# Loading two rows of an output projection through GpSimd's queue, in pieces of 57 and 38 partitions

## The chip, the core and the metric

The kernel runs on one core of one Trainium2 chip. The metric is the device time of one execution in microseconds; the time of the kernel before is the median of three runs. A core has five engines that matter here: TensorE (PE), VectorE (DVE), ScalarE (ACT), GpSimd (POOL) and SyncE (SP). Transfers between the chip's memory (HBM) and the core's memory (SBUF) are made by sixteen DMA engines; a transfer is put into a queue by an instruction on SP, ACT or POOL.

## The reference

Grouped-query attention of 8 sequences with 4 new tokens each, against caches of 2,048 keys and values, between two projections. All inputs are bf16.

```python
B, Sq, D = 8, 4, 512
Hq, Hkv, Sk, Dh = 32, 8, 2048, 128
# x (B,Sq,D)  k_cache, v_cache (B,Hkv,Sk,Dh)  wq (D,Hq*Dh)  wo (Hq*Dh,D)
q = (x @ wq).reshape(B, Sq, Hq, Dh).transpose(0, 2, 1, 3)
k = jnp.repeat(k_cache, Hq // Hkv, axis=1)
v = jnp.repeat(v_cache, Hq // Hkv, axis=1)
scores = jnp.einsum("bhqd,bhkd->bhqk", q, k) * (Dh ** -0.5)
o = jnp.einsum("bhqk,bhkd->bhqd", softmax(scores), v)
out = o.transpose(0, 2, 1, 3).reshape(B, Sq, Hq * Dh) @ wo
```

The caches are 32 MB (of 1,048,576 bytes) each, wq and wo 4 MB each, so that nearly all of the traffic is read once.

## The kernel before

The work is cut into eight units, u = 0 to 7. A unit is 4 MB of keys and 4 MB of values: units 1 to 6 are one sequence with all its eight heads, units 0 and 7 are half of the heads of the last two sequences. SBUF holds a ring of four slots of 4 MB (`ring`, 128 partitions of 32 KB in each slot). All large loads go into the ring in a fixed order: k0, wq, k1, v0, k2, v1, k3, v2 and so on to v6, v7, wo. `take` deals the slots round, so wo, the eighteenth load, gets the slot that v5 had.

For one unit, DVE transposes the keys (`turn`, L213), PE multiplies them with the queries (`scores`, L251), DVE finds the maximum (L264), ACT takes the exponentials (L291), DVE transposes them (L305), and ACT and POOL copy them into a block-diagonal tile (`p_bd`, L315). One unit later PE multiplies these with the values (`values`, L331). In the program's order, pass u of the main loop (L442) holds the scores of unit u and the values of unit u - 1, and ends with `issue(2 + 2 * u)` (L472), which puts into the queues the loads whose slots are free by then. The transfer that follows in a queue waits, on the issuing engine, until the last reader of its slot is done. Pass 6 issues wo, so wo waits for `values(5, 1)`.

The loads are issued by SP, but for one half of k0, which is issued by ACT. `load_kv` (L110) makes one DMA of a whole 4 MB unit, or two. A unit named in the list `split` (L155) is cut by member, that is into the two halves of each partition's 32 KB in SBUF; for values these are two groups of four heads. v7 is cut another way, into halves of the keys. A V load cut by member and a whole one read the same runs of 16 KB in HBM.

`load_wo` (L141) sees wo as two halves, gg = 0 and 1, each of 128 partitions with sixteen rows of 512 numbers (1 KB a row, so 16 KB in one run for each partition). The first half is one DMA of sixteen rows; the second is cut into rows 0 to 7, 8 to 12, 13 to 14, and 15.

At the end `project` (L399) multiplies the attention's result with wo, row by row, two matmuls for a row: the first half's rows 0 to 3, then its rows 4 to 15, then the second half's rows 0 to 15 (L476 to L480). Each row waits for the DMA that brought it. The result is then copied by DVE and ACT (L482, L483) and stored by SP (L484).

The tile `pad` (128 partitions of 192 numbers, L72) stands ahead of the ring in SBUF. The kernel before neither writes nor reads it.

Of the kernel before, what the change touches and what calls it, by code (L numbers as in the profile page):

```python
# [17 lines left out]
def kernel(  # L18
# [9 lines left out]
    nc = tc.nc  # L28

    B, Sq, D = x.shape  # L30
# [11 lines left out]
    NU = B * Hkv // (G * NB)  # L42
# [11 lines left out]
    RW = 16  # L54
# [17 lines left out]
    pad = ring_pool.tile([128, 192], BF16, name="pad")  # L72
    ring = ring_pool.tile([128, NR, NB, C * Dh], BF16, name="ring")
# [27 lines left out]
    def take(key):  # L101
        slot_of[key] = n_loads[0] % NR
        n_loads[0] += 1
        return slot_of[key]
# [30 lines left out]
    def load_wq():  # L135
# [2 lines left out]
            ring[:, slot, :, :].rearrange("p b n -> p (b n)"), wq.rearrange("(p r) n -> p (r n)", r=R)  # L138
        )

    def load_wo():  # L141
        slot = take("wo")
        for gg, cuts in ((0, (0, RW)), (1, (0, 8, 13, 15, RW))):
            rows = wo[gg * G * 512 : (gg + 1) * G * 512, :].rearrange("(p r) j -> p (r j)", r=RW)
            for r0, r1 in zip(cuts, cuts[1:]):
                nc.sync.dma_start(ring[:, slot, gg, r0 * D : r1 * D], rows[:, r0 * D : r1 * D])

    loads = ["k0", "wq", ("k", 1)]
    for u in range(NU):
# [2 lines left out]
            loads.append(("k", u + 2))  # L152
    loads.append("wo")
    loads.reverse()
    split = [("v", 0), ("v", 1), ("v", 2), ("v", 3), ("v", 4), ("k", NU - 1)]  # L155

    def issue(done):

        while loads and n_loads[0] < done + NR:
            what = loads.pop()  # L160
            if what == "k0":
                load_kv("k", 0, by_member, (nc.sync, nc.scalar))
                nc.sync.dma_start(x_sb[:, :], x.flatten_outer_dims())
            elif what == "wq":
                load_wq()
            elif what == "wo":
                load_wo()
            elif what in split:
                load_kv(*what, by_member)
            else:  # L170
                load_kv(*what, by_half if what == ("v", NU - 1) else whole)
# [343 lines left out]
```

## Time and profile before

| what | value |
|---|---|
| median of three runs | 184.73 us (184.65 to 189.89) |
| the profiled execution, own time | 184.38 us |
| its span, first to last instruction | 182.5 us |
| mean granted TensorE clock | 0.963 |
| PE, DVE, ACT, POOL busy | 136.6, 128.7, 70.3, 39.3 us |
| moved by DMA | 75.70 MB, mean 415 GB/s |
| chain that ended last | DMA 42%, DVE 23%, PE 22% |

All times in the views are of the profiled execution, in microseconds from the start of its span. A DMA is cut into packets, one for each contiguous run of one partition; the packets are dealt to the DMA engines. The trace has, for each packet, its queue, size, start and duration, and for each DMA the sixteen times at which its completion semaphore was raised, without the engine's name. The packets of kind "instruction" bring instructions to the engines' own memories; the kernel does not issue them. Queue 1 is SP's.

### The profile page before, as it was taken

To read this page: it belongs to the slowest core of one execution; us is meant where nothing else is said; L and a number is where in the kernel's file an instruction comes from. 1 tells how busy PE (TensorE), PEld (TensorE's weight loads), DVE (VectorE), ACT (ScalarE), POOL (GpSimd) and SP (SyncE) were. 2 spreads that over 40 slices of the span, in tenths; PEclk is the share of its full clock that TensorE was granted. 3 is DMA by queue.
4 is the path that set the end of the run, shared out by engine and by line. 5 is a ranking of instruction groups with operands and counts; after the bars stand their busy time and mean duration, and the time that the engine had idled before them with its cause. 6 is when DMAs were issued, how large, how long until landed. Compare 5 with 4: busy or idle time off the path is not lost.

```text
span 182.5 us, 2386 instructions
## 1 busy us (share of the span) xinstructions
PE 136.6 (75%) x924; PEld 83.3 (46%) x924; DVE 128.7 (71%) x161; ACT 70.3 (39%) x91; POOL 39.3 (22%) x110
## 2 busy tenths in 40 slices
PE   0000076940999999998999898989399977899993
PEld 0000022310348635843783485358234852388971
DVE  6518025738994999599689957995399559967340
ACT  2000020019604940990395079109900792063010
POOL 8800006006200700430080035004400220023000
PEclk9999999995589999999999999999969999999999
DMA  6999999999999998999999999999999999999991
GB/s 226 431 485 395 424 460 406 424 445 449 452 384 427 456 461 382 420 460 452 391 417 453 460 402 418 431 478 424 391 435 424 435 427 435 415 426 438 427 385 42
DMA packets 4938, 75.70 MB, mean 415 GB/s; under 512 B 512, under 2 KB 704, under 8 KB 960
## 3 DMA queue, kind: packets, MB, share of 16 engines
q1 hardware_dynamic: 4784, 73.47, 94.3%
q10 hardware_dynamic: 144, 2.10, 2.8%
q8 instruction: 7, 0.11, 0.2%
q14 instruction: 3, 0.02, 0.0%
HBM read 75.53 MB, written 0.03 MB: 414 GB/s over the span
## 4 chain that ended last, share of the span: by engine, by line
DMA 42%; DVE 23%; PE 22%; issue 4%; ACT 3%; POOL 2%; SPq 1%; ACTq 0%; DVEq 0%; POOLq 0%
DMA ring<-in_wo_dram 16%; PE s_ps L251 16%; DMA ring<-in_k_cache_dram 15%; DVE kt L213 14%; DMA ring<-in_wq_dram 12%; DVE stat L264 4%; PE o_ps L331 4%; ACT p_sb L291 3%; PE psq L425 2%; DVE pt L305 2%; DVE stat L322 1%; POOL p_bd L315 1%; POOL q_bd L231 1%; PE s_ps L403 1%; DVE stat L272 0%
## 5 line engine op out<-in xcount | busy, mean ns | idle before, releaser
L251 PE MATMUL s_ps<-kt,q_bd 128*128 128x512 bf16 x256 | 69.5, 409 | 20.0 <-POOL q_bd L231 9.9
L213 DVE STREAM_TRANSPOSE kt<-ring 128x1024 f32<-128x1024 f32 x64 | 73.9, 1210 | 14.2 <-DMA ring<-in_k_cache_dram 11.4
L331 PE MATMUL o_ps<-ring,p_bd 128*128 128x256 bf16 x512 | 57.2, 273 | 0.0
L251 PEld LDWEIGHTS <-q_bd 128*128 128x128 bf16 x256 | 25.3, 102 | 63.0 <-issue 26.6
L331 PEld LDWEIGHTS <-p_bd 128*128 128x128 bf16 x512 | 49.8, 98 | 6.0 <-issue 0.2
L315 ACT COPY p_bd<-pt 32x1024 bf16<-32x1024 bf16 x44 | 45.8, 1041 | 1.5 <-DVE pt L305 1.1
L291 ACT ACTIVATE p_sb<-s_ps,stat 128x1024 bf16<-128x1024 f32 x16 | 17.7, 1110 | 72.2 <-DVE stat L272 72.2
L315 POOL COPY p_bd<-pt 32x1024 bf16<-32x1024 bf16 x16 | 17.0, 1065 | 105.9 <-DVE pt L305 93.2
L264 DVE TENSOR_REDUCE stat<-s_ps 128x1 f32<-128x1024 f32 x16 | 19.3, 1208 | 3.4 <-PE s_ps L251 3.4
L305 DVE STREAM_TRANSPOSE pt<-p_sb 128x512 f32<-128x512 f32 x16 | 11.4, 712 | 14.0 <-ACT p_sb L291 14.0
L231 POOL COPY q_bd<-qT 32x64 bf16<-32x64 bf16 x64 | 13.1, 231 | 20.7 <-DVE qT L436 19.0
L425 PE MATMUL psq<-ring,xT_sb 128*32 128x512 bf16 x32 | 3.6, 630 | 9.1 <-DMA ring<-in_wq_dram 9.1
L416 PE MATMUL xtp<-ident,x_sb 32*128 32x32 bf16 x4 | 0.3, 195 | 13.3 <-DMA x_sb<-in_x_dram 13.3
L436 DVE STREAM_TRANSPOSE qT<-q_sb 128x64 f32<-128x64 f32 x8 | 1.2, 214 | 8.8 <-ACT q_sb L432 8.8
L177 DVE MEMSET p_bd<- 128x2048 uint32 x3 | 5.3, 1765 | 2.0 <-PEq L499 1.2
L322 DVE TENSOR_SCALAR stat<-of_b,stat 128x2 f32<-128x2 f32 x8 | 6.3, 793 | 0.3
L416 PEld LDWEIGHTS <-x_sb 32*128 32x128 bf16 x4 | 0.2, 117 | 13.3 <-DMA x_sb<-in_x_dram 13.3
L425 PEld LDWEIGHTS <-xT_sb 128*32 128x32 bf16 x32 | 1.3, 140 | 10.5 <-issue 10.1
L432 ACT CAST q_sb<-psq 128x512 bf16<-128x512 f32 x2 | 1.2, 586 | 11.8 <-PE psq L425 11.8
L375 PEld LDWEIGHTS <-perm 128*128 128x128 bf16 x56 | 3.8, 97 | 2.0 <-issue 0.5
L419 ACT COPY xT_sb<-xtp 128x128 bf16<-128x128 bf16 x1 | 0.3, 266 | 11.2 <-PE xtp L416 11.2
L343 ACT ACTIVATE o_sb<-o_ps,stat 128x128 bf16<-128x128 f32 x8 | 2.9, 368 | 4.1 <-PE o_ps L331 3.9
(30 smaller groups left out, 46.4 us busy)
## 6 DMA issues: line engine op xcount, KB each, us to landing
ring<-in_k_cache_dram SPq DMA_DIRECT2D x6, 4096.0 KB, 22.7
ring<-in_v_cache_dram SPq DMA_DIRECT2D x12, 2048.0 KB, 23.6
ring<-in_v_cache_dram SPq DMA_DIRECT2D x2, 4096.0 KB, 29.6
ring<-in_k_cache_dram SPq DMA_DIRECT2D x3, 2048.0 KB, 27.2
ring<-in_wq_dram SPq DMA_DIRECT2D x1, 4096.0 KB, 21.0
ring<-in_k_cache_dram ACTq DMA_DIRECT2D x1, 2048.0 KB, 12.4
ring<-in_wo_dram SPq DMA_DIRECT2D x1, 2048.0 KB, 25.9
ring<-in_wo_dram SPq DMA_DIRECT2D x1, 1024.0 KB, 28.2
```

The source lines that it names most:

```text
L177: nc.vector.memset(t[:, :, :, :, :], 0.0)
L213: nc.vector.transpose(out=out, in_=in_)
L231: nc.gpsimd.tensor_copy(out=qb[k * 32 : (k + 1) * 32, m, :, g, b, :].rearrange("w (j e) q -> w j e q", e=2), in_=qT[of * 32 : (of + 1) * 3 ...
L251: nc.tensor.matmul(s_ps[t // 2][:, t % 2, :], lhsT=q_bd[u % 2][:, m, 2 * j + e, :, :, :].rearrange("w g b q -> w (g b q)"), rhs=rhs, start ...
L264: nc.vector.tensor_reduce(out=stats[u][0][:, h : h + 1], in_=s_ps[h][:, :, :].rearrange("q t n -> q (t n)"), axis=AX, op=ALU.max, negate=True,
L291: nc.scalar.activation(out=out, in_=in_, func=EXP, bias=stats[u][1][:, :], scale=scale, accum_out=stats[u][2][:, h : h + 1],)
L305: nc.vector.transpose(out=pt[:, :, :, :].rearrange("s c q e -> s (c q e)").bitcast(FP32), in_=ps[u, h][:, :, :, :].rearrange("q c s e -> q ...
L315: copy(out=pb[rows, :, g, :, :], in_=pt[rows, :, :, :])
L322: nc.vector.tensor_scalar_mul(stats[u][3][:, :], of_b[:, :], stats[u][4][:, :])
L331: nc.tensor.matmul(o_pss[u][:, :, :], lhsT=pbs[u, h][:, i // 2, :, :, i % 2].rearrange("s g q -> s (g q)"), rhs=v[:, :, key_of(u, h, i // ...
L375: nc.tensor.matmul(o_pms[r // 2][:, r % 2, gg, :], lhsT=perm[:, r, w : w + 128], rhs=o_sbs[u][:, b, :], start=(u == 0 and r % 2 == 0 and g ...
L425: nc.tensor.matmul(psq[g * T : (g + 1) * T, :], lhsT=xT_sb[:, r, :], rhs=w[:, (g * NB + gg) * rep * Dh : (g * NB + gg + 1) * rep * Dh], st ...
```

## The change

The first half of wo is no longer one DMA. Rows 0 to 13 are loaded by SP as before. Rows 14 and 15, which make one run of 2 KB for each partition, are cut by partitions: 0 to 56 (57 partitions) and 57 to 94 (38) are issued by GpSimd, 95 to 126 (32) and 127 (one) by SP. Ahead of each GpSimd piece stands a short load by GpSimd too, `load_rows`, of 6 and of 5 rows of x with 24 bytes each, into `pad`, which still nobody reads. The second half is cut as before. Also v3 and v4 leave the list `split`, so that each of them is loaded by one DMA of 4 MB instead of two of 2 MB.

```diff
+    def load_rows(n):
+
+        nc.gpsimd.dma_start(pad[:n, 16 * n : 16 * n + 12], x.flatten_outer_dims()[:n, :12])
+
     def load_wo():
         slot = take("wo")
-        for gg, cuts in ((0, (0, RW)), (1, (0, 8, 13, 15, RW))):
+
+        def load(engine, gg, p0, p1, r0, r1):
             rows = wo[gg * G * 512 : (gg + 1) * G * 512, :].rearrange("(p r) j -> p (r j)", r=RW)
-            for r0, r1 in zip(cuts, cuts[1:]):
-                nc.sync.dma_start(ring[:, slot, gg, r0 * D : r1 * D], rows[:, r0 * D : r1 * D])
+            engine.dma_start(ring[p0:p1, slot, gg, r0 * D : r1 * D], rows[p0:p1, r0 * D : r1 * D])
+
+
+        RL, PA, PB = RW - 2, 57, 57 + 38
+        load(nc.sync, 0, 0, 128, 0, RL)
+        load_rows(6)
+        load(nc.gpsimd, 0, 0, PA, RL, RW)
+        load_rows(5)
+        load(nc.gpsimd, 0, PA, PB, RL, RW)
+        load(nc.sync, 0, PB, PB + 32, RL, RW)
+        load(nc.sync, 0, PB + 32, 128, RL, RW)
+        for r0, r1 in ((0, 8), (8, 13), (13, 15), (15, RW)):
+            load(nc.sync, 1, 0, 128, r0, r1)
...
-    split = [("v", 0), ("v", 1), ("v", 2), ("v", 3), ("v", 4), ("k", NU - 1)]
+    split = [("v", 0), ("v", 1), ("v", 2), ("k", NU - 1)]
```

## The prediction

> **What bounds the kernel now.** I read the page's slices and queues first, then the chain that ended last, then the timeline of the last 35 us, and last the completion records.
>
> The page's DMA lines (busy tenths in 40 slices; then queue, packets, MB, share of 16 engines' span):
>
> ```profile
> span 182.5 us, 2386 instructions
> PE   0000076940999999998999898989399977899993
> DMA  6999999999999998999999999999999999999991
> q1 hardware_dynamic: 4784, 73.47, 94.3%
> q8 instruction: 7, 0.11, 0.2%
> ```
>
> The DMA engines are full from the second slice to the last but one; SP's queue q1 fills nearly all of that. No other row is as full.
>
> The chain that ended last (start us, us, what), its end:
>
> ```profile
> 148.45 0.34 SPq L146
> 148.79 0.05 issue
> 148.84 0.42 SPq L146
> 149.27 0.05 issue
> 149.32 29.10 DMA ring<-in_wo_dram
> 178.42 0.04 issue
> 178.46 0.27 PE s_ps L403
> ...
> 179.71 0.40 DVE out_sb L482
> ```
>
> The wo pieces are issued from 148.45 and land up to 29 us later: they stand behind a backlog, so when they are issued matters little, and what the engines still have to move matters. In the timeline (start us, us, engine, line) POOL has little there:
>
> ```profile
> 144.77 2.14 POOL L315 COPY p_bd<-pt 32x1024 bf16<-32x1024 bf16 x2 [14.49 <-DVE pt L305]
> 163.22 1.23 POOL L315 COPY p_bd<-pt 32x1024 bf16<-32x1024 bf16 x1 [16.31 <-DVE pt L305]
> ...
> 178.46 0.27 PE L403 MATMUL s_ps<-ring,oP 128*32 128x256 bf16 x1 [0.34 <-DMA ring<-in_wo_dram]
> ...
> 180.17 0.35 SPq L484 DMA_DIRECT2D out_dram<-out_sb  x1
> ```
>
> PE reaches row 8 of wo's second half and waits for a transfer; POOL is idle from 146.9 to 163.2.
>
> Each load leaves sixteen completion marks in the trace, one for each DMA engine, without the engine's name. For the last wo load (row 15 of the second half), us after the first mark at 177.54:
>
> ```
> 0 .19 .37 .38 .44 | .66 .67 .78 .81 | 1.50 1.52 1.65 1.66 1.77 1.79 1.81
> ```
>
> The last comes at 179.35, PE's last matmuls start at 179.39, and the span ends 3.1 us after that mark. So **five engines lead, four are between, seven lag**, and the seven decide. Where they come from is in the same records: up to 51.7 us the spread is 0.7 us; each of the seven 16 KB records of q8 (starting 53.9, 74.8, 93.5, 116.4, 139.7, 163.3 and 175.0) is followed by one more engine that stays about 1.1 us behind (1 at 57.6, 2 at 77.3, 4 at 120.8, 7 at 179.35). No engine is hit twice.
>
> **What each part costs.** SP's packets in the steady stretch take 611 ns for 16,384 B, 309 for 8,192, 196 for 5,120, 84 for 2,048, 46 for 1,024 and 9 for a 4 B mark: 8 ns and 36.8 ns per 1,000 B. A packet of 14,336 B then is 536 ns.
>
> - Shortening the first half's load from sixteen rows to fourteen: each engine has 8 of its 128 packets, so 8 x (611 - 536) = -0.60 us on every engine.
> - The load of 32 partitions: 2 packets of 2,048 B on each engine, 2 x 84 = +0.17. x, also 32 rows, left 2 packets for each of 16 marks. The load of one partition is +0.08 on one engine.
> - The GpSimd pieces, 57 and 38 packets of 2,048 B. No row shows a load from this queue. The rows of SP's loads are dealt in equal shares (128 as 16 x 8, 32 as 16 x 2). Equal shares of 57 on at most 16 engines means 1 or 3 engines, and of 38 it means 1 or 2; as many as possible gives 3 and 2, **nineteen packets each, 19 x 84 = +1.60 on five engines**. The bounds are 4 + 3 packets on nearly every engine (+0.59) and all 57 on one engine (+4.79); I take nineteen as nearest to the even dealing of the rows.
> - The short loads of x: 6 and 5 packets of 24 B, at most 46 ns each by the nearest row; +0.02 on eleven engines. Dealt in turn, 6, 3, 5 and 2 engines make sixteen, so no engine gets two pieces. Their data goes into pad, which nobody reads.
> - Marks: four GpSimd loads, 4 x 9 = +0.04. The two V loads whole instead of split save 2 x 9 ns, the two new SP loads add 2 x 9. The packets of these V loads stay 16 KB and both members are read by the same matmuls, so else it is nothing.
>
> Sum: the eleven other engines -0.60 + 0.17 + 0.04 + 0.02 = -0.38; the five -0.60 + 0.17 + 0.04 + 1.60 = +1.20.
>
> On the spread, if the five are the leaders: 0 to .44 become 1.20 to 1.64, the laggards 1.43 at most, the middle 0.43. The last mark moves from 1.81 to 1.64: **-0.17 us**. PE passes this on: its waits for wo after 177.85 add up to more (0.34 us before 178.46 alone).
>
> The Trainium skill's page "DMA: Bandwidth & Descriptors", section "Why a DMA increments its semaphore by 16 and not by 1", gives the same 3 and 2 (the largest divisor up to 16) and lets GpSimd's queue deal to consecutive engines from a cursor that goes round; no run here shows it yet. The same sentence speaks of an exception, a rival below.
>
> **What lies beside other work.** SP issues seven wo loads instead of five and two fewer V loads; two issues of 0.4 us are hidden by the 26 to 29 us of backlog. SP's loads use eight semaphores in turn; moved on by the new loads, the last two wo issues would take those of v6 and of v7's first half, which landed at 159.76 and 164.64. If SP waits for them, only the output's DMA is behind (180.17), and the pieces are still 13 us ahead of their landing; with no backlog left this would be on the path whole. POOL gains a **wait** for values(5) to free the slot (PE's last read ends at 148.44), then four issues. Behind it is only the p_bd copy at 163.22, for which values(7) waits; 14.8 us cover it. No row prices a POOL issue; against SP's 0.4 us it would need 3.7 us each to show, so I take nothing; without the cover each us is an us for that copy. The early bytes (190 KB) are moved ahead of v6 and v7. On leaders this only uses up their lead (v6's leaders at 157.89 plus 1.6 is 159.5, before the last mark at 159.76). PE must observe four loads instead of one before rows 14 and 15 of the first half, some tenths of a us at most, covered by the waits it now has at 178.46.
>
> The Trainium skill speaks against such a change in the same page's "Rules for kernel authors": spreading loads over SP, ACT and GpSimd brings no bandwidth, since all use the same sixteen engines. The trace agrees that the engines are full (1.00 from 30 to 165 us); by that rule alone the sum would be zero, since it is about the total and not about who is late.
>
> **Rivals.** (1) *The five engines are not the leaders.* The marks don't name engines, and five drawn blindly from sixteen would avoid all seven laggards in 126 of 4,368 draws. Then a laggard ends at 1.50 + 1.20 = 2.70 to 1.81 + 1.20 = 3.01: +0.9 to +1.2 us, 185.3 to 185.6, and v6 and v7 land as much later. It decides as soon as one engine at 0.61 or later is among the five (0.61 + 1.20 = 1.81). Against it: the extra of 1.60 is near the distance between the groups (means 0.28 and 1.67), and the short loads can serve nothing but the choice of engines. Should the fetches or the dealing start elsewhere from run to run, this is the usual case.
> (2) *The pieces go evenly over the engines.* 4 + 3 packets: -0.60 + 0.17 + 0.04 + 0.59 = +0.20, 184.6. The exception named above (the Trainium skill, same section: some plain GpSimd copies get 16 engines with the rounded-up share) would do just this. The rows of 128 and 32 can't tell it from equal shares, but they don't show an uneven share either.
> (3) *One engine takes a whole piece.* -0.38 + 4.79 = +4.41 on one engine: 0.44 + 4.41 - 1.81 = +3.0 on a leader, +4.4 on the last laggard: 187.4 to 188.8. For it: nothing but that no row excludes it.
> (4) *A GpSimd issue costs far more than SP's* and p_bd's copy comes late: from 14.8 us on, us for us. A lead of 0.7 us (everything levelled at the mean of 1.00 plus 0.11) is the most that the other side could give: 183.7.
>
> **How the numbers follow.** The sum is made against the profiled execution's own 184.38 us (span 182.5 and 1.9 around it), 0.35 below the median of 184.73. Forecast 184.38 - 0.17 = **184.2**, chance 0.55, its own range 183.8 to 184.6 (packets on the new queue 20% dearer add 0.3; full levelling takes 0.5 more). Rival 1 at 0.28, 2 at 0.08, 3 at 0.05, 4 and the rest at 0.04. From 183.8 to 185.6 holds forecast and rivals 1 and 2 but for their edges. A measurement of this kernel can tell about 2% from no change, 3.7 us. Over 2% slower takes rival 3 on a late engine or rival 4: 0.05. Over 2% faster nothing here gives; 0.02 for what I don't see. Within 2%: 0.93.
>
> **What would show it.** Right: the last load's marks no longer fall in groups of five, four and seven but within some 1.2 us with four at the front; the four POOL loads issued between 148.5 and 155 and landed before 160; the POOL copy still at 163; the tail of 3.1 us after the last mark unchanged. Wrong: two or more marks over 2.5 us behind the first (rival 1), the old groups with all of them 0.2 later (2), one mark 4 us behind (3), or values(7) waiting for POOL (4).

## The result and the profile after

The changed kernel takes **185.75 us** (median), the kernel before 184.71 in the same comparison; the ratio is 1.0055, with a 95% interval of 1.0042 to 1.0068. That is 1.0 us slower: within 2%, but clear of noise, on the other side of the forecast of 184.2 and just above the range. In a second comparison of the same kernel the ratio was 1.0144 (1.0126 to 1.0162), 2.6 us.

The first profile after the change is of an execution of 191.93 us, in which packets were slower between 13 and 66 us already; so the lines below are from the second profile of the same kernel (187.14 us), and of four experiments (wo alone, no short loads, the pieces by SP, the even pieces by SP) only the times from 140 us on are used. First what the DMA engines moved in the 40 slices of the kernel before:

```profile
GB/s 226 431 485 395 424 460 406 424 445 449 452 384 427 456 461 382 420 460 452 391 417 453 460 402 418 431 478 424 391 435 424 435 427 435 415 426 438 427 385 42
```

and the page after the change (the slices, then the queues):

```profile
span 185.3 us, 2393 instructions
DMA  6999999999999999999999999999999999999991
GB/s 223 439 471 439 425 396 435 435 460 439 393 421 442 467 433 387 425 460 439 400 432 432 446 419 425 471 410 417 439 421 428 439 415 406 376 386 396 364 361 38
q1 hardware_dynamic: 4802, 73.27, 94.0%
q0 software_dynamic: 160, 0.20, 0.3%
```

The DMA engines are as full as before, and the bytes are the same, but from the 34th slice on they move less: 361 to 406 GB/s, where the kernel before has 385 to 438. q0 is GpSimd's queue. The windows of the same stretches show when that begins (us from the start, the engines' busy time, granted clock, DMA share, GB/s); the kernel before:

```profile
142.00:152.00 10.00, 7.89 (x66) 6.25 (x65) 6.06 (x10) 8.81 (x11) 2.08 (x2) 1.00 1.01 431
152.00:162.00 10.00, 9.16 (x54) 4.65 (x53) 8.90 (x10) 0.93 (x1) 0.00 (x0) 1.00 0.99 422
162.00:172.00 10.00, 10.00 (x98) 9.02 (x96) 6.28 (x12) 4.19 (x8) 2.45 (x2) 1.00 1.03 435
172.00:177.00 5.00, 4.65 (x59) 3.80 (x58) 2.12 (x6) 0.74 (x2) 0.00 (x0) 1.00 0.97 401
```

and the changed kernel:

```profile
142.00:152.00 10.00, 7.89 (x67) 6.37 (x66) 6.05 (x10) 8.80 (x11) 4.23 (x6) 1.00 1.02 434
152.00:162.00 10.00, 7.91 (x42) 3.40 (x40) 9.14 (x10) 0.69 (x1) 0.00 (x0) 1.00 0.99 386
162.00:172.00 10.00, 10.00 (x95) 8.96 (x94) 5.50 (x10) 4.06 (x7) 2.58 (x2) 1.00 1.03 394
172.00:177.00 5.00, 3.98 (x41) 3.46 (x39) 1.89 (x3) 0.74 (x2) 0.00 (x0) 1.00 1.00 360
```

The DMA share is 1.0 in all of them, so no engine ran dry; each packet took longer. Up to 152 us the two kernels agree (431 and 434 GB/s). The timeline says what starts then (POOL's queue, start and length in us):

```profile
148.97 0.54 POOL L150 DMA_DIRECT2D ring<-in_wo_dram  x1 [1.24 <-PE o_ps L347]
149.50 0.51 POOL L143 DMA_DIRECT2D pad<-in_x_dram  x1
150.00 0.53 POOL L150 DMA_DIRECT2D ring<-in_wo_dram  x1
163.39 1.29 POOL L331 COPY p_bd<-pt 32x1024 bf16<-32x1024 bf16 x1 [12.87 <-DVE pt L321]
```

The first piece of wo is issued at 148.97, its packets run from 152.8. In the packet records SP's packets of 16,384 B take about 681 ns instead of 611 from 157 us on, and those of 8,192 B about 342 instead of 309, up to 177 us. I sum this up as the **excess**: what SP's packets from 140 us on took beyond 8 ns and 36.8 ns per 1,000 B, divided by sixteen engines. It is 0.07 us in the kernel before and 2.49 in this profile. The chain of waits ends as before, only later:

```profile
150.32 30.81 DMA ring<-in_wo_dram
181.13 0.04 issue
181.17 0.27 PE s_ps L419
...
182.39 0.40 DVE out_sb L498
```

The last wo mark comes at 182.03 (before: 179.35), the marks of that load are spread over 1.85 us (before: 1.81), seven engines still lag, and the tail after the last mark is 3.2 us.

### The profile page after: what moved, and what is told of

It reads as the page before. It is cut to its first block, busy times and chain, and to the rows that moved or that the text cites. A ratio compares the mean times of both kernels' runs of the same rounds, so it can differ in the third digit from the quotient of the medians.

```text
span 190.0 us, 2393 instructions
## 1 busy us (share of the span) xinstructions
PE 137.0 (72%) x924; PEld 83.6 (44%) x924; DVE 128.9 (68%) x161; ACT 70.2 (37%) x91; POOL 41.5 (22%) x114
## 4 chain that ended last, share of the span: by engine, by line
DMA 57%; PE 17%; DVE 17%; issue 3%; POOL 2%; ACT 2%; SPq 1%; ACTq 0%; POOLq 0%; DVEq 0%
DMA ring<-in_k_cache_dram 29%; DMA ring<-in_wo_dram 16%; DVE kt L229 13%; DMA ring<-in_wq_dram 12%; PE s_ps L267 10%; PE o_ps L347 4%; PE psq L441 2%; ACT p_sb L307 1%; DVE stat L280 1%; POOL p_bd L331 1%; DVE pt L321 1%; SPq L150 1%; POOL q_bd L247 1%; PE s_ps L419 1%; DVE stat L338 0%
## 5 line engine op out<-in xcount | busy, mean ns | idle before, releaser
L419 PE MATMUL s_ps<-ring,oP 128*32 128x256 bf16 x32 | 4.3, 272 | 0.7 <-DMA ring<-in_wo_dram 0.6
```

Of the source, the lines that this page charges most:

```text
L419: nc.tensor.matmul(out_ps[half], lhsT=oP[gg][:, r, :], rhs=w[:, r, half * DH : (half + 1) * DH], start=(gg == 0 and r == 0), stop=(gg == N ...
```

## The experiments

All ratios are to the kernel before on the same chip, with the 95% interval. The first four ask which part costs.

**The whole change again.** No edit.

> The whole change again, for a profile that can be laid beside the one of before. Packet records of the first profile after the change show the 57 rows dealt as four rows each on fourteen engines and one on a fifteenth, the 38 as three each on twelve and two on one. Theory A (the GpSimd queue is the cost: the pieces are dealt almost evenly, so no laggard is relieved, and the packets and marks of that queue cost more engine time than the 0.20 us of rival 2): about 1.0055, the last wo mark some 1 us later against the start than before, and the delay appears between 150 and 165 us, when that queue's packets run. Theory B (the whole V loads are the cost): the same ratio, but the loads after v3 and v4 already land about 0.8 us later than before, between 90 and 125 us. Theory C (the two last wo loads are issued later because SP waits): the same ratio, with a gap in the DMA engines' work after 175 us.

1.0144 (1.0126 to 1.0162). The landings up to 150 us agree with those of before within 0.3 us, so the whole V loads (theory B) are out. SP's wo issues, before (first line) and in this run (second line):

```profile
148.45 7.75 SPq L146 DMA_DIRECT2D ring<-in_wo_dram  x5
148.58 18.39 SPq L150 DMA_DIRECT2D ring<-in_wo_dram  x7
```

SP now needs 18.39 us to get through them, as the prediction's order of semaphores has it, but there is no gap after 175 us: the pieces still land in order with the engines full, so theory C is out too.

**Only the V loads whole.**

```diff
-    split = [("v", 0), ("v", 1), ("v", 2), ("v", 3), ("v", 4), ("k", NU - 1)]
+    split = [("v", 0), ("v", 1), ("v", 2), ("k", NU - 1)]
```

> Only v3 and v4 are loaded whole; wo as in the kernel before. Theory A: 1.000 (0.999 to 1.001), since the same packets move. Theory B: about 1.0045, +0.8 us, with the landings after v3 later. Theory C: 1.000.

1.0004 (0.9991 to 1.0017). By itself this part is nothing.

**Only wo in the new way.** The change without the edit above.

> Only wo is loaded in the new way; v3 and v4 stay split. Theory A: the whole loss, about 1.0055. Theory B: about 1.001, +0.2 us from the even dealing. Theory C: the whole loss.

1.0084 (1.0066 to 1.0102): the loss is in wo's load. Its excess is 0.88 us, in two stretches: 0.5 while GpSimd's packets run and 0.3 where SP's pieces of 32 and 1 partitions pass. The whole change cost 1.0144 beside it, though the V loads alone cost nothing. Whether the two parts act on each other is not shown: the same whole change gave 1.0055 in the first comparison, so one kernel differs by as much from one comparison to the next.

In this experiment and in all that follow v3 and v4 are split as in the kernel before, and each diff shows only the lines that load rows 14 and 15 of the first half of wo, against the changed kernel or, where it has the loop over `cuts`, against the kernel before.

**The cut without the second queue.**

```diff
-        for gg, cuts in ((0, (0, RW)), (1, (0, 8, 13, 15, RW))):
+        for gg, cuts in ((0, (0, RW - 2, RW)), (1, (0, 8, 13, 15, RW))):
```

> The first half of wo is cut into rows 0 to 13 and rows 14 and 15, both by SP over all 128 partitions: the cut without the other queue; v3 and v4 split. Each engine gets 8 packets of 14,336 B and 8 of 2,048 B for 8 of 16,384 B, 8 x (536 + 84 - 611) ns + one mark = +0.08 us. Theory A and B: 1.0005, all the rest being the queue or the V loads. Theory C: SP issues one load more, so one late issue of the two remains; a part of the loss, about 1.002.

1.0004 (0.9991 to 1.0018), excess 0.07. Shorter packets as such cost what the prediction said, and the stream keeps its rate where these rows pass (172 to 177 us, before 401 GB/s):

```profile
172.00:177.00 5.00, 4.65 (x56) 3.80 (x56) 2.12 (x5) 0.74 (x2) 0.00 (x0) 1.00 0.99 405
```

The packet records of the changed kernel also tell how the pieces were dealt. GpSimd's queue made packets of up to 4,096 B, two rows each, where SP's queue makes one of each row. Of the 57 rows, fifteen engines got their first packet within 1 us; there were 28 packets of two rows and one of a single row, which is four rows on each of fourteen engines and one on a fifteenth. The 38 became 13 packets of two rows and 12 of one: three rows on each of twelve engines, two on another. So at most twelve engines got seven rows, nobody got more, and nobody got nineteen. The next question was what makes the packets slow: a second queue (theory Q) or the shape of the pieces (theory S).

**Without the short loads of x** (wo as in the change, v3 and v4 split, the two `load_rows` calls left out).

> v3 and v4 split as before; wo in the new pieces, but without the two short loads of x. In the profile of the whole change, SP's packets take 10% longer from the moment when GpSimd's queue runs (16,384 B in 681 ns instead of 611), for 24 us; in that of wo alone for shorter stretches. Theory Q (any larger load on a second queue throws the engines' packets out of step, and they stay slow until something puts them back) and theory S (it is the shape of the pieces, whose partitions are dealt to other engines than SP's loads of 128): as wo alone, 1.005 to 1.013. Theory D (the short loads matter, by moving on which engines get the pieces): another loss than that, below 1.003 or above 1.015.

1.014 (1.0026 to 1.0253), a wide interval; excess 0.86, again in two stretches. The short loads are not needed for the loss.

**Only the short loads.**

```diff
         load_rows(6)
-        load(nc.gpsimd, 0, 0, PA, RL, RW)
         load_rows(5)
-        load(nc.gpsimd, 0, PA, PB, RL, RW)
-        load(nc.sync, 0, PB, PB + 32, RL, RW)
-        load(nc.sync, 0, PB + 32, 128, RL, RW)
+        load(nc.sync, 0, 0, 128, RL, RW)
```

> The two short loads of x stay on GpSimd's queue, and rows 14 and 15 of the first half are loaded by SP over all 128 partitions. Theory Q in its strict form (any packet on a second queue does it): a slow stretch, 1.004 or more. Theory Q for larger loads only, and theory S: 1.0005 as with the cut by SP alone.

1.0013 (0.9997 to 1.0029), excess 0.07. The six packets of 24 B of the first short load start at 150.751, .901, .996, 151.078, .113 and .343; the five of the second at 151.977, 152.126, .222, .339 and .569, each 1,225 or 1,226 ns after one of the first six, two of SP's packets later. They went to five of the same six engines: a short load does not move the next one on to other engines.

**GpSimd's queue with an even load of 128 partitions.**

It stands in place of the four pieces and the short loads.

```diff
+        load(nc.gpsimd, 0, 0, 128, RL, RW)
```

> Rows 14 and 15 of the first half are one load of 128 partitions by GpSimd, no short loads: the second queue with the even shape of SP's loads. Engine work: 8 x (536 - 611) + 4 x 168 ns + marks = +0.1 us. Theory Q: SP's packets slow down beside and after it, 1.004 to 1.013. Theory S: 1.001.

1.0002 (0.9989 to 1.0015): **a second queue alone costs nothing.** Its 64 packets of 4,096 B took 159 ns each, excess 0.08, and the windows are those of before (422 and 435 GB/s):

```profile
152.00:162.00 10.00, 8.56 (x48) 4.04 (x47) 9.07 (x10) 0.76 (x1) 0.00 (x0) 1.00 0.99 422
162.00:172.00 10.00, 10.00 (x98) 9.02 (x96) 5.69 (x11) 4.36 (x8) 2.58 (x2) 1.00 1.03 434
```

Theory Q is out.

**The pieces by ACT's queue** (`nc.scalar` for `nc.gpsimd`, no short loads).

> The pieces of 57 and 38 partitions are issued by ACT instead of GpSimd, no short loads. If this queue deals equal shares (nineteen packets on each of three and of two engines), and always from the same first engine on, two engines get both pieces: -0.40 + 3.20 = +2.8 us on them, so 1.4 us (on leaders) to 2.8 us (on laggards) later, 1.008 to 1.015; if it deals like GpSimd's, 1.001 and what theory Q or S add. Theory Q and S both expect SP's packets to be slow beside it; only theory Q expects them to stay slow after it.

1.0194 (1.0117 to 1.0272). Three engines had one of these packets every 687 ns, in three phases that stay fixed up to 156 us, and each got nineteen: this queue does deal equal shares, and the 38 went to two engines. In the last load's marks two engines stand 3.1 and 3.6 us behind the first, the others within 2.0. The excess of 1.83 us comes on top and begins only about 157 us, after several rounds.

Three more kernels separate the shares from the partitions.

**The same pieces, all by SP** (`nc.sync`, no short loads).

> The pieces of 57, 38, 32 and 1 partitions are all issued by SP, no second queue and no short loads. ACT's queue dealt the 57 as nineteen packets on each of three engines and the 38 on two of the same engines. If SP's deals alike, two engines have 2.8 us more, as with ACT. Theory U (uneven shares move the engines' packets against each other, and then they run slower, whatever the queue): slow stretches without any second queue, 1.012 to 1.02. Theory Q2 (uneven pieces do it only beside another queue): SP's packets keep 611 and 309 ns, and only the engine work is left, 1.007 to 1.010.

1.0178 (1.0115 to 1.0242), excess 1.40 in one stretch of about 5 us; the 2,048 B packets took up to 155 ns instead of 84. No second queue is needed for slow packets. The page counts 534 packets under 512 B, 22 more than before. These are the marks of the four pieces, 16 + 3 + 2 + 1, so SP's queue dealt the 57 to three engines and the 38 to two, as ACT's did.

**Even pieces, by SP and by GpSimd.** The lines by SP, in place of the four pieces and the short loads; in the second kernel `nc.gpsimd` issues the first of the two.

```diff
+        load(nc.sync, 0, 0, 96, RL, RW)
+        load(nc.sync, 0, 96, 128, RL, RW)
```

> Rows 14 and 15 by SP in pieces of 96 and 32 partitions: 6 + 2 packets on every engine, an even share, but with other partitions on an engine than in a load of 128. Engine work as with the plain cut, +0.09 us with one more mark. Theory U: 1.0005, no slow stretch. Theory M (the other partitions do it: two engines meet at one place in SBUF or HBM): a slow stretch of about 10% while these packets run, some 0.1 us in 1 us, and as long after as it stays; 1.001 to 1.005.

> As the even pieces by SP, but the 96 partitions are issued by GpSimd: 6 packets on each engine, beside v6. Theory U: about 1.0005, like GpSimd's load of 128, and SP's packets keep their 611 ns but for some tens of ns. Theory M: slow while the 96 packets run, 10% or more over 3 us, 0.3 us or more, 1.002 to 1.008.

1.0072 (1.0043 to 1.0101) by SP and 1.0070 (1.0041 to 1.0099) with the 96 by GpSimd. **Theory U is out: both pieces have marks from all sixteen engines (544 packets under 512 B, 32 more than before), so the shares are even, and the packets are slow all the same.** By SP the excess is 0.96 us, all of it while these 128 packets run: 84 ns for the first 59 of them, then up to 162. By GpSimd it is 1.29: 0.59 beside the 96 (153 to 156 us) and 0.65 from 173 to 178 us, where the 32 pass. In between, the packets have their old times, as the windows of this kernel show:

```profile
152.00:162.00 10.00, 8.73 (x42) 3.98 (x41) 8.90 (x10) 0.79 (x1) 0.00 (x0) 0.83 0.99 393
162.00:172.00 10.00, 10.00 (x97) 9.00 (x95) 5.50 (x10) 3.96 (x7) 2.58 (x2) 1.00 1.02 430
172.00:177.00 5.00, 4.65 (x52) 3.78 (x49) 1.89 (x3) 0.75 (x3) 0.00 (x0) 1.00 1.01 377
```

393 GB/s beside the 96, 430 without a piece, 377 beside the 32.

**All partitions, other rows of HBM.** Rows 14 and 15 in one SP load, in place of the four pieces and the short loads. Partition 8b + a gets the wo rows of partition 16a + b, so the result is a sum over other rows than the reference's:

```diff
+        turned = wo[: G * 512, :].rearrange("(a b r) j -> b a (r j)", b=16, r=RW)
+        nc.sync.dma_start(
+            ring[:, slot, 0, RL * D : RW * D], turned[:, :, RL * D : RW * D]
+        )
```

> Rows 14 and 15 of the first half are one SP load into all 128 partitions, but partition 8b + a takes the wo rows that belong to partition 16a + b, so the result is a sum over other rows than the reference's. SBUF is written in an even load over all partitions, HBM is read in another order by each engine. Theory M on the HBM side (an engine that reads other addresses than in a load of 128 meets another engine's): the 2,048 B packets take 100 to 160 ns instead of 84 and the loss is as with the even pieces by SP, 1.004 to 1.007. Theory M on the SBUF side (two engines write to partitions that lie together): 84 ns and 1.0004, as with the plain cut, as long as engine and partitions stay paired as in a plain load.

1.0085 (1.0068 to 1.0102). Even shares, all 128 partitions, and still 84 ns turned into up to 208, excess 1.19:

```profile
162.00:172.00 10.00, 10.00 (x98) 9.01 (x97) 6.09 (x12) 4.34 (x8) 2.45 (x2) 1.00 1.02 430
172.00:177.00 5.00, 4.30 (x51) 3.50 (x50) 1.75 (x4) 0.74 (x2) 0.00 (x0) 1.00 1.00 323
```

323 GB/s where the kernel before has 401. This speaks for the HBM side, but it does not settle it. The edit also moves the rows that neighbouring partitions read from 16 KB to 256 KB apart, which the pieces do not, so its slow packets may have another cause than theirs. The Trainium skill's page "DMA: Bandwidth & Descriptors", section "The descriptor swizzle", pairs engine 0 of a plain load of 128 with partitions 0 to 3 and 32 to 35; this load is seen as 16 x 8 and may be dealt eight partitions in a row, and no record names the partition that an engine wrote.

**x ahead of the first keys**, in the kernel before: x is its one load of fewer than 128 partitions.

> The kernel before, with x, its only load of fewer than 128 partitions, issued ahead of the first keys instead of behind them, so that no other load runs beside its 32 packets. If only the shape of a load beside others costs, x costs little where it stands (its packets take 46 ns, and nothing in the profile of before is slow beside it), and the ratio is 1.000 (0.998 to 1.002). If x beside the keys sets off slow packets, as the pieces of wo do, faster: below 0.998.

1.0045 (1.0032 to 1.0057), slower, as neither side expected. x now has the queue to itself, and its marks come from 2.14 to 3.92 us; behind it the sixteen engines start the keys one after the other, and the marks of the following loads are spread over 1.1 us instead of 0.7. Where x stood, its 32 packets took 46 ns each and no packet beside them is slow. So not every load of fewer than 128 partitions slows the stream, and what sets x apart from the piece of 32 is open.

## Why the prediction was wrong

**The step that failed** is the dealing of the GpSimd pieces. It took equal shares as nearest to SP's rows and put nineteen packets on each of five engines. The packet records show the rounded-up share on nearly all engines, which was its bound of 4 + 3 packets and its second rival. The Trainium skill's page "DMA: Bandwidth & Descriptors", section "Why a DMA increments its semaphore by 16 and not by 1", has this as an exception for plain GpSimd copies, and the trace agrees with the exception. Equal shares do hold on ACT's and SP's queues, as the runs by ACT and by SP show. With the rows spread like this no laggard is relieved: in the last load of the second profile nine marks come within 0.82 us and seven 1.44 to 1.84 us behind the first, so the gain of 0.17 us is gone.

**The second rival had the dealing right and its size wrong.** It priced engine work alone, +0.20 us. The larger part of the miss is a term that was missing from the sum, and from the bounds of the price of a packet: the neighbours' packets get slower, 0.5 us beside GpSimd's pieces and 0.3 beside SP's 32 and 1 in the profile of wo alone. In the second comparison the slow packets lasted for 24 us; its 2.49 - 0.07 + 0.20 = 2.6 us is the 2.6 measured, and there the profile is of one of the executions that were timed. The sum does not close everywhere: 0.20 + 0.8 is 1.0 us, the size of the first result, but that profile is of wo alone, whose own ratio of 1.0084 is 1.6 us. No profile shows the first comparison's executions of 185.5 to 185.8 us, so how its 1.0 us is made up is not shown. How long the slow packets last differs from kernel to kernel and from one comparison to the next, and what ends them is not shown by any run here. That the upper end of the range, 185.6 by rival 1, came near the result is luck: no engine got the nineteen packets that rival 1 puts on it.

**The rest, step by step.** That the DMA engines bound the end, and that the last mark plus a tail of 3.1 us is the end of the span, held (3.2). The shortening of the packets held: the cut by SP alone cost 0.08 us by the working and 1.0004 on the chip. The whole V loads at nothing held. The two more SP issues and the wait for a semaphore stayed hidden, although SP needed 18.39 us for them: the last two pieces were issued 20.4 and 15.4 us ahead of their landing. POOL's wait was hidden as reasoned: the four issues took 0.51 to 0.64 us each, were done at 150.5, and the p_bd copy started at 163.39. Rival 3 did not come: no engine got a whole piece.

**The argument that misled** was that the extra of 1.60 us fitted the distance between the groups. A size that would fit is no row for where the packets go; on that point the trace of before had nothing, as the text said, and the forecast still gave it 0.55.

## What to carry to other kernels

On a stream that already fills the sixteen DMA engines, cutting a load by partitions (96 + 32, or 57 + 38 + 32 + 1) made packets 10% or more slower in every run that did it, 0.9 to 2.5 us of excess in a kernel, while cutting it by rows over all 128 partitions cost 0.0004 of the time, which is within the noise. Why the packets get slow is not shown. Before a load is used to shift work between engines, look in the packet records at how that queue deals its rows: GpSimd's queue deals the same shape differently from ACT's and SP's. When the share of busy DMA time stays at 1.0 and the GB/s fall, ask what the packets' durations are, not who waits.

## What the runs showed of the hardware

- GpSimd's queue dealt 57 rows as 14 x 4 + 1 and 38 as 12 x 3 + 2; ACT's dealt 57 as 3 x 19 and 38 to two engines, and SP's put as many marks to these pieces (22 for the four). Two short GpSimd loads in a row went to the same engines.
- GpSimd's queue put two rows of 2,048 B into one packet of 4,096 B (159 ns, or 80 ns a row); SP's and ACT's queues made a packet of each row (84 ns).
- A second queue of the same even shape beside SP's stream cost nothing (1.0002), and a POOL issue took 0.51 to 0.64 us.
- Packets of 2,048 B took 84 ns in a plain load of 128 partitions, up to 162 in pieces of 96 and 32, and up to 208 with other rows of HBM. The first packets of each such load still took 84 ns (59 of 128 in the pieces by SP).
